# Three score tiles beside each other in four PSUM banks of one tile, key transposes at its ends, and weight conversions behind the first batch

## The chip, the core and the metric

One core of a Trainium2 chip runs the whole program. The metric is the time of one execution on the device in microseconds (us), as the median of several runs; the profile is one more execution, recorded instruction by instruction. Five engines run their own queues in order: PE (TensorE, matrix products; its weight loads are listed as PEld), DVE (VectorE), ACT (ScalarE), POOL (GpSimd) and SP, which here only issues DMAs.

## What is computed

Attention over 8 batches and 8 heads of 576 tokens with 64 features, in which only scores within `tau` of their row's maximum are kept, then a gated feed-forward layer over all 4608 tokens.

```python
scores = scale * np.matmul(q, k.transpose(0, 1, 3, 2))
thresh = np.max(scores, axis=-1, keepdims=True) - tau
scores = np.where(scores >= thresh, scores, -1000000000.0)
scores = scores - np.max(scores, axis=-1, keepdims=True)
attn = np.exp(scores)
attn = attn / (np.sum(attn, axis=-1, keepdims=True) + 1e-09)
...
gate = 1.0 / (1.0 + np.exp(-(x @ w_gate)))
val = x @ w_val
return (gate * val @ w_out).astype(np.float32)
```

All inputs are float32; `x` is the attention's output, 4608 x 512, and the weights are 512 x 1536 (twice) and 1536 x 512.

## The kernel before

**Attention** goes in 32 visits, one for each batch and pair of heads (names such as `5_1` are batch 5, pair 1). A visit has nine score tiles of 128 queries x 576 keys: four for each head and one, called `l`, for the 64 left-over queries of both heads. `tile_steps` (L571) makes one tile: PE writes the scores into a PSUM tile `s` in two halves of 288 keys (L591 for the first batch, in plain float32; L599 after it, in two or three products of split operands); DVE takes the row maximum (`st`, L606); POOL or DVE makes the threshold (L615); ACT writes the exponential of the scores into `p` (L620); DVE reads the scores again and masks `p` with the threshold, with the row sum on the side (L623). Then POOL scales `p` (L657), PE turns it in blocks (`tp`, L668; the 64 left-over keys of a group apart, `lk`, L681), ACT or DVE copies these out of PSUM (`pt` and `pl`, L630 and L631), and PE multiplies with the values (`av`, L704).

**Feed-forward.** Blocks 0, 1 and 2 run as plain products (`m`, L764, then `o`, L807) that fill PE beside the attention. The other six blocks of tokens run behind the attention in three pairs by a seven-product scheme (`q` chains at L1006, `r` chains at L1071), with three PSUM accumulators a, b and c for each chain and DVE sums at L943 and L945.

**Conversions.** The 36 weight tiles are unpacked from the host's form by POOL, ACT and DVE (`convert`, L384), written to DRAM and read again as products need them. 12 of the 24 tiles of `w_gate` and `w_val` are kept in SBUF for block 0 (`OWN`); the other 12 are read again (`wi_0a`, `wi_1a`).

**PSUM** has eight banks of 512 float32 columns for each partition. Before, `s` has two buffers of two banks each (the b accumulators of the seven-product scheme use them as well), and four single banks `b` serve everything else, `lk` among it.

**What sets the order.** The kernel first lists all operations with a priority key and a cost, and a planner (`Plan.run`) lets five queues take what is ready and has room; the resulting order is emitted as straight code. `LEAD`, `LAG`, `SHIFT`, `CONV_IN` and the costs steer it. A layer below the kernel then adds the waits: where an instruction touches a tile that an instruction of another engine has touched and the two must not overlap, the later one in the emitted order waits on a semaphore of the earlier one's engine. The planner knows buffers, but not these waits.

## Time and profile before

| what | us |
|---|---|
| three runs, median | 1356.05 |
| three runs, lowest to highest | 1355.28 to 1359.21 |
| span of the profiled execution, first to last instruction | 1352.1 |

The span leaves out what lies around it, such as the launch; against the median these are 3.95 us. Times within the profile count from the span's start. A row of a group has the line, engine, operation, tile written and tiles read, shapes, count, then busy us and mean ns of one, then the idle time ahead of it and who ended it. A row of a timeline has start, duration, engine, line, operation, and how many instructions it merges.

### The profile page before, as it was taken

How to read it: one execution, taken by the hardware profiler on the slowest of the kernel's cores; microseconds unless marked ns; L12 is line 12 of the kernel's file. 1: busy time of each engine (PE TensorE's matmuls, PEld its weight loads, DVE VectorE, ACT ScalarE, POOL GpSimd, SP SyncE). 2: the span in 40 equal slices, each digit the busy share in tenths (PEclk: the TensorE clock that was granted, in tenths of full speed). 3: DMA queues.
4: the chain of work that ended last, by engine and by line, in shares of the span. 5: the costliest groups of instructions: out<-in, count | busy, mean ns of one | idle time of the engine just before them, and what ended most of it. 6: DMA issues, size and time to landing. Idle time of an engine off the chain costs nothing.

```text
span 1352.1 us, 23686 instructions
## 1 busy us (share of the span) xinstructions
PE 1320.8 (98%) x8292; PEld 1084.1 (80%) x8292; DVE 954.8 (71%) x1943; ACT 726.9 (54%) x1339; POOL 630.3 (47%) x660
## 2 busy tenths in 40 slices
PE   7879999999999999999999999999999999999998
PEld 4557888888888888888888878888888888888887
DVE  7889868567877777778787763556965569654594
ACT  7878766666766766667776653223532225322242
POOL 6985957956777764967776741101000110001100
PEclk8989999999999999999999999999999999999999
DMA  9879999897978988898897858656695656756564
GB/s 341 279 251 309 311 257 269 233 279 209 264 212 242 261 242 227 250 267 238 238 270 188 241 179 295 205 180 211 201 308 183 201 193 204 249 180 204 186 221 129
DMA packets 140436, 317.83 MB, mean 235 GB/s; under 512 B 22048, under 2 KB 49952, under 8 KB 140320
## 3 DMA queue, kind: packets, MB, share of 16 engines
q1 hardware_dynamic: 140176, 316.33, 76.5%
q8 instruction: 67, 1.10, 0.4%
q14 instruction: 49, 0.40, 0.1%
q10 hardware_dynamic: 144, 0.00, 0.0%
HBM read 210.37 MB, written 54.53 MB: 196 GB/s over the span
## 4 chain that ended last, share of the span: by engine, by line
PE 87%; DMA 6%; DVE 2%; ACT 2%; issue 1%; POOL 1%; SPq 1%; ACTq 0%; DVEq 0%; POOLq 0%
PE m L764 13%; PE qb L1006 11%; PE av L704 11%; PE s L599 8%; PE qc L1006 7%; PE qa L1006 7%; PE tp L668 7%; PE o L807 6%; PE rb L1071 5%; PE rc L1071 4%; PE ra L1071 4%; DMA wo<-wod 2%; DMA kd<-k 2%; PE s_l L599 1%; PE lk L681 1%
## 5 line engine op out<-in xcount | busy, mean ns | idle before, releaser
L657 POOL TENSOR_SCALAR p<-p,zero_t,sm 128x576 f32<-128x576 f32 x256 | 216.3, 856 | 107.9 <-DVE sm L655 76.5
L606 DVE TENSOR_REDUCE st<-s 128x1 f32<-128x576 f32 x256 | 192.3, 754 | 91.9 <-PE s L599 83.2
L623 DVE SCALAR_TENSOR_TENSOR p<-s,st,p 128x576 f32<-128x576 f32 x256 | 205.9, 812 | 30.2 <-ACT p L620 23.9
L620 ACT ACTIVATE p<-s,st 128x576 f32<-128x576 f32 x256 | 190.2, 750 | 57.4 <-DVE st L606 56.5
L919 POOL TENSOR_TENSOR gA<-gA 128x512 f32<-128x512 f32 x18 | 24.1, 1341 | 416.2 <-DVE gA L985 416.2
L630 ACT COPY pt<-tp 128x512 f32<-128x512 f32 x256 | 147.4, 589 | 54.0 <-PE tp L668 51.9
L599 PE MATMUL s<-kd,qd 128*128 128x288 f32 x896 | 165.0, 308 | 3.7 <-issue 1.6
L668 PE MATMUL tp<-ident,p 128*128 128x128 f32 x1024 | 156.7, 282 | 2.5 <-POOL p L657 2.0
L764 PE MATMUL m<-x,wi 128*128 128x512 f32 x576 | 158.9, 403 | 0.0
L668 PEld LDWEIGHTS tp<-ident,p 128*128 128x128 f32 x1024 | 123.2, 143 | 29.4 <-POOL p L657 7.6
L599 PEld LDWEIGHTS s<-kd,qd 128*128 128x128 f32 x896 | 133.9, 190 | 14.6 <-DVE p_l L623 2.4
L704 PE MATMUL av<-pt,vs 128*64 128x256 f32 x1024 | 126.1, 389 | 0.0
L807 PE MATMUL o<-g,wo 128*128 128x512 f32 x432 | 117.5, 401 | 0.0
L943 DVE TENSOR_TENSOR qu<-qb,qp 128x512 f32<-128x512 f32 x72 | 49.8, 692 | 89.9 <-PE qb L1006 77.1
L764 PEld LDWEIGHTS m<-x,wi 128*128 128x128 f32 x576 | 99.9, 189 | 14.3
L1006 PE MATMUL qa<-xs_p,wa 128*128 128x512 f32 x432 | 109.6, 389 | 0.0
L704 PEld LDWEIGHTS av<-pt,vs 128*64 128x64 f32 x1024 | 68.6, 138 | 48.5 <-issue 7.5
L1006 PEld LDWEIGHTS qa<-xs_p,wa 128*128 128x128 f32 x432 | 81.1, 188 | 16.8
L807 PEld LDWEIGHTS o<-g,wo 128*128 128x128 f32 x432 | 75.5, 189 | 10.9
L630 ACT COPY xf<-av 128x256 f32<-128x256 f32 x64 | 25.6, 399 | 77.4 <-PE av L704 73.1
L911 ACT CAST gs_p<-gA 128x512 fp32r<-128x512 f32 x54 | 32.4, 620 | 64.5 <-DVE gA L985 26.5
L981 ACT ACTIVATE gA<-qa 128x512 f32<-128x512 f32 x18 | 10.8, 598 | 103.4 <-PE qa L1006 103.4
(148 smaller groups left out, 2628.3 us busy)
## 6 DMA issues: line engine op xcount, KB each, us to landing
kd<-k SPq DMA_DIRECT2D x112, 320.0 KB, 6.0
wi<-wid SPq DMA_DIRECT2D x48, 512.0 KB, 6.9
wo<-wod SPq DMA_DIRECT2D x36, 512.0 KB, 7.0
wa<-wid SPq DMA_DIRECT2D x36, 512.0 KB, 4.1
ws<-sid SPq DMA_DIRECT2D x36, 512.0 KB, 4.5
wt<-sid SPq DMA_DIRECT2D x36, 512.0 KB, 3.3
wo_p<-sod SPq DMA_DIRECT2D x36, 512.0 KB, 4.6
qd<-q SPq DMA_DIRECT2D x112, 128.0 KB, 4.6
```

The costliest lines, as they stand in the source:

```text
L599: nc.tensor.matmul(s.ap[:, c, :HALF], st(), mv(slice(kc + c * HALF, kc + (c + 1) * HALF)), start=m == 0, stop=m == len(steps) - 1,)
L606: op("DVE", 0.76, key, lambda: nc.vector.tensor_reduce(out=st.ap[:, 0:1], in_=sv(), axis=AX.XY, op=ALU.max, negate=True), reads=[s], write ...
L620: op("ACT", 0.74, key, lambda: nc.scalar.activation(p(), sv(), AF.Exp, bias=st.ap[:, 0:1], scale=1.0), reads=[s, (st, 0)], writes=[(g.p, i)])
L623: op("DVE", 0.9, key, lambda: nc.vector.scalar_tensor_tensor(out=p(), in0=sv(), scalar=st.ap[:, 1:2], in1=p(), op0=ALU.is_ge, op1=ALU.mult ...
L630: return op("ACT", act(n), key, lambda: nc.scalar.copy(dst(), src.ap), reads=[src], writes=[part])
L657: op("POOL", 0.9, key, lambda i=i: nc.gpsimd.tensor_scalar(out=p.ap[:, i * S : (i + 1) * S], in0=p.ap[:, i * S : (i + 1) * S], scalar1=zer ...
L668: nc.tensor.matmul(tp.ap[:, c, :], self.p.ap[:, o + c * P : o + (c + 1) * P], ident, is_transpose=True, start=c == 0, stop=c == NJ - 1, sk ...
L704: nc.tensor.matmul(av.ap[h * D : (h + 1) * D, a:z], vis.vs.ap[:, j, h], m(h), start=i == 0, stop=i == len(ms) - 1, skip_group_check=True,)
L764: nc.tensor.matmul(m.ap, wv[:, a, c * P : (c + 1) * P], xs[c].ap[:, z, c0:c1], start=e == 0, stop=e == 11,)
L807: nc.tensor.matmul(acc.ap, wv[:, f, a], g[fg * ND + f].ap[:, z], start=(fg, f, a, z) == (0, 0, 0, 0), stop=(fg, f, a, z) == (NFG - 1, ND - ...
L1006: nc.tensor.matmul(acc.ap, wv[:, y, (2 * h + c) * P : (2 * h + c + 1) * P], xt[prod][c].get()[:, z], start=e == 0 and prod in FIRST, stop= ...
L1071: nc.tensor.matmul(acc.ap, w.ap[:, e, c, y], gt[prod][2 * g + c].get()[:, z], start=m == 0 and g == 0 and prod in FIRST, stop=m == 5 and g ...
```

## The change

- PSUM: instead of two `s` buffers of two banks each, one tile `shared` of 2048 columns in four banks. A score tile takes one of three places of 576 columns, side by side from column 160 on: 160 to 736, 736 to 1312, 1312 to 1888. The first place lies in banks 0 and 1, the second in 1 and 2, the third in 2 and 3. Each tile is written in two pieces that end at a bank border (352 and 224, 288 and 288, 224 and 352 columns). The left-over key transposes `lk` go to the 128 columns at either end of `shared`; the b accumulators take whole banks of it. The planner hands out places (`settle`). Readers now see the 576 columns of a tile in one run.
- The first batch's keys are stored whole in both halves of the partitions, since a piece may now start anywhere (`k0`, `SK` columns for each tile instead of 352).
- Conversions get later keys (`CONV_IN`), all 24 tiles of `w_gate` and `w_val` stay in SBUF for block 0 (`OWN` 24, `w` 10 buffers), the second batch is put 20 tiles later in key (`SHIFT`), the scores of a visit are held behind a unit of the feed-forward layer in the planner's order (`held_by`, `RATE`, `SLACK`), and `LEAD`, `LAG` and `THR_UNTIL` have new numbers.

```diff
...
     def __init__(self, plan, tag, shape, dtype, name, cls=None):
         self.plan, self.tag, self.shape, self.dtype, self.name, self.cls = plan, tag, shape, dtype, name, cls
-        self.t, self.accesses, self.users, self.held = None, [], 0, False
+        self.t, self.accesses, self.users, self.held, self.place = None, [], 0, False, None
         self.turn = plan.made[tag] = plan.made.get(tag, 0) + 1
     @property
...
     def __init__(self, pools, slots):
         self.pools, self.slots = pools, slots
         self.ops, self.held, self.made, self.given = [], {}, {}, {}
+        self.homes, self.live = {}, {}
     def buf(self, tag, shape, dtype, name, cls=None):
         return Buf(self, tag, shape, dtype, name, cls)
     def make(self, b):
+        if b.place is not None:
+            return self.shared[:, b.place[0] : b.place[1]]
         pool, bufs = self.pools[b.tag]
         return pool.tile(b.shape, b.dtype, tag=b.tag, name=b.name, bufs=bufs)
...
                 return False
+        if not self.settle([b for s in need.values() for b in s]):
+            return False
...
+    def settle(self, bufs):
+
+        taken = list(self.live.values())
+        places = {}
+        for b in bufs:
+            if b.tag not in self.homes:
+                continue
+            n = b.shape[-1] if b.tag != "s" else self.homes["s"][0][1] - self.homes["s"][0][0]
+            for c0, c1 in self.homes[b.tag]:
+                if all(c1 <= x or y <= c0 for x, y in taken):
+                    places[b] = (c0, c1)
+                    taken.append((c0, c1))
+                    break
+            else:
+                return False
+        for b, at in places.items():
+            b.place = self.live[b] = at
+        return True
     def run(self):
         engines = ("PE", "DVE", "ACT", "POOL", "SP")
...
                     for b in x.bufs:
                         b.users -= 1
                         if not b.users and b.held:
+                            self.live.pop(b, None)
                             self.held[b.tag] -= 1
                             self.held[b.tag, b.cls] -= 1
                     for s in x.succ:
...
 SLOTS = {
     "kn": 1, "qn": 1, "vn": 1, "k2": 1, "q2": 1, "kd": 3, "qd": 3, "vs": 3,
     "p": 3, "pc": 1, "sm": 8, "st": 16, "pt": 2, "pl": 2, "ptc": 1, "plc": 1, "xf": 2, "x": 5, "g": 12,
-    "w": 8, "t2": 6,
+    "w": 10, "t2": 6,
 }
-LEAD = 8
-CONV_IN, CONV_OUT = (10, 1.5), (56, 3)
+LEAD = 7
+CONV_IN, CONV_OUT = (30, 2.5), (56, 3)
 EARLY = 16
...
     return "ACT"
-THR_FIRST, THR_UNTIL, LK_UNTIL = "POOL", 36, 300
+THR_FIRST, THR_UNTIL, LK_UNTIL = "POOL", 90, 300
 def TP(g, i):
...
-OWN = 12
-
-SHIFT = 50
+OWN = 24
+
+SHIFT = 70
 def LO_DVE(j, out):
...
 DVE_LO_IN, DVE_LO_OUT = range(18,24), ()
-LAG = {"PE": 1.2, "DVE": 0.3, "ACT": 0.08, "POOL": 0.3, "SP": 0.08}
+LAG = {"PE": 1.5, "DVE": 0.3, "ACT": 0.08, "POOL": 0.3, "SP": 0.08}
 WARM = 16
+
+RATE, SLACK = 3, 3
 FIRST_PAIRS = 4
 KD_COST = 1.2
...
     nc.vector.tensor_scalar(out=scale_t, in0=tau_t, scalar1=0.0, scalar2=QSCALE, op0=ALU.is_ge, op1=ALU.mult)
-    warm = ps.tile([P, 2, SM], F32, tag="s", name="warm")
+    shared = ps.tile([P, NJ * SM], F32, tag="shared", name="shared", bufs=1)
...
     pools = {t: (sb, n) for t, n in SLOTS.items()}
-    pools["s"], pools["b"] = (ps, 2), (ps, 4)
+    pools["s"], pools["e"], pools["q"], pools["b"] = (ps, 3), (ps, 2), (ps, 4), (ps, 4)
     slots = {t: n for t, (_, n) in pools.items()}
     active = {"att": 1, "moe": 0}
...
     last_att = [None]
     plan = Both(pools, slots)
+    plan.shared = shared
+    SIDE = (NJ * SM - 3 * S) // 2
+    plan.homes = {
+        "s": [(SIDE + i * S, SIDE + (i + 1) * S) for i in range(3)],
+        "e": [(0, P), (NJ * SM - P, NJ * SM)],
+        "q": [(i * SM, (i + 1) * SM) for i in (0, 2, 1, 3)],
+    }
     op, buf = plan.op, plan.buf
     def dram(shape, name):
...
         def plain_scores(self, key, n):
             pair = 4 * self.b + self.hp
-            self.k1 = [buf("qd", [P, HALF + SL], F32, f"kp{n}_{h}") for h in range(2)]
+            self.k1 = [buf("qd", [P, SK], F32, f"kp{n}_{h}") for h in range(2)]
             qn = self.q1 = buf("kd", [P, 2, S], F32, f"qp{n}")
             pieces = [(0, 2 * P), (2 * P, S)] if n == "0_0" else [(0, S)]
...
         n = f"{g.name}{i}"
-        s = buf("s", [P, 2, SM], F32, f"s{n}")
+        s = buf("s", [P, S], F32, f"s{n}")
         kc = SL if i == 0 else 0
-        sv = lambda: s.ap[:, :, :HALF]
+        sv = lambda: s.ap
         cols = None if h is None else slice(qt * P - vis.c0, (qt + 1) * P - vis.c0)
         if vis.plain_s:
...
             ]
             reads = [vis.qd[h], vis.kd[h]]
+        def pieces():
+            c0, c1 = s.place
+            at = -(-c0 // SM) * SM - c0
+            assert c0 + at < c1 and SL <= at and max(at, S - at) <= HALF + SL
+            return (0, at), (at, S)
+
         def plain_scores():
-            for (x, c0, r0, r1), c in itertools.product(heads, range(2)):
+            for (x, c0, r0, r1), (a, z) in itertools.product(heads, pieces()):
+                c = (s.place[0] + a) // SM % 2
                 rows = slice(c * D, (c + 1) * D)
                 nc.tensor.matmul(
-                    s.ap[r0:r1, c, :HALF], vis.q1.ap[rows, x, c0 : c0 + r1 - r0],
-                    vis.k1[x].ap[rows, kc : kc + HALF], start=True, stop=True, skip_group_check=True,
+                    s.ap[r0:r1, a:z], vis.q1.ap[rows, x, c0 : c0 + r1 - r0],
+                    vis.k1[x].ap[rows, kc + a : kc + z], start=True, stop=True, skip_group_check=True,
                 )
         def scores():
             for m, (st, mv) in enumerate(steps):
-                for c in range(2):
+                for a, z in pieces():
                     nc.tensor.matmul(
-                        s.ap[:, c, :HALF], st(), mv(slice(kc + c * HALF, kc + (c + 1) * HALF)),
+                        s.ap[:, a:z], st(), mv(slice(kc + a, kc + z)),
                         start=m == 0, stop=m == len(steps) - 1,
                     )
-        op("PE", 0.8 if vis.plain_s else len(steps) * 2 * mm(HALF), key, plain_scores if vis.plain_s else scores, reads=reads, writes=[s], also=[g.p])
+        op("PE", 0.8 if vis.plain_s else len(steps) * 2 * mm(HALF), key, plain_scores if vis.plain_s else scores, reads=reads, writes=[s], also=[g.p], after=held_by(vis))
         st = buf("st", [P, 2], F32, f"st{n}")
         op("DVE", 0.76, key, lambda: nc.vector.tensor_reduce(
-            out=st.ap[:, 0:1], in_=sv(), axis=AX.XY, op=ALU.max, negate=True
+            out=st.ap[:, 0:1], in_=sv(), axis=AX.X, op=ALU.max, negate=True
         ), reads=[s], writes=[(st, 0)])
         thr = THR(vis.first)
         if thr == "ACT":
...
                 out=st.ap[:, 1:2], in0=st.ap[:, 0:1], scalar1=-1.0, scalar2=ntau_t[:, 0:1],
                 op0=ALU.mult, op1=ALU.add,
             ), reads=[(st, 0)], writes=[(st, 1)])
-        p = lambda: g.p.ap[:, i * S : (i + 1) * S].rearrange("p (a c) -> p a c", a=2)
+        p = lambda: g.p.ap[:, i * S : (i + 1) * S]
         op("ACT", 0.74, key, lambda: nc.scalar.activation(
             p(), sv(), AF.Exp, bias=st.ap[:, 0:1], scale=1.0
         ), reads=[s, (st, 0)], writes=[(g.p, i)])
...
         if e == "ACT":
             return op("ACT", act(n), key, lambda: nc.scalar.copy(dst(), src.ap), reads=[src], writes=[part])
         return op("DVE", dve(n), key, lambda: nc.vector.tensor_copy(dst(), src.ap), reads=[src], writes=[part])
+
+    def held_by(vis):
+        n = RATE * (4 * vis.b + vis.hp - 4) - SLACK
+        return [unit_ends[n]] if 0 <= n < len(unit_ends) else []
     class Group:
...
         def leftover_keys(self, key):
-            lk = buf("b", [P, P], F32, f"lk{self.name}", "att")
+            lk = buf("e", [P, P], F32, f"lk{self.name}")
             o = SM if self.n == 2 else S - P
             op("PE", 0.14, key, lambda: nc.tensor.matmul(
                 lk.ap, self.p.ap[:, o : o + P], ident, is_transpose=True
...
     def chains(n, scale, done, tag):
-        ps_ = {c: buf("s" if c == "b" else "b", [P, SM], F32, f"{tag}{c}{n}", "moe") for c in "abc"}
+        ps_ = {c: buf("q" if c == "b" else "b", [P, SM], F32, f"{tag}{c}{n}", "moe") for c in "abc"}
         t = {c: buf("pc" if c == "u3" and not (tag == "r" and n.endswith("_1")) else "t2", [P, SM], F32, f"{tag}{c}{n}") for c in ("p1", "u2", "u3")}
         def plus(bank, x, out):
...
```

How the built program changes is shown at three places around the start of visit 5_1, in the middle of the attention. A row has the line, the operation, tile written and tiles read, the shape, and the engines whose semaphores it waits on (a wait that an earlier one covers is not repeated). The number at a name's end only counts names. `s5_1_000` is a score tile of visit 5_1 (head 0, first group, first tile), `s5_1_l40` that of its left-over queries, and `shared_84` the new PSUM tile.

DVE before, from the maximum of visit 5_1's first tile on (a maximum writes `st`, a mask `p`):

```order
L606 TENSOR_REDUCE st5_1_000_7079<-s5_1_000_7070 128x1 [waits PE_49]
L615 TENSOR_SCALAR st5_1_000_7079<-st5_1_000_7079,ntau_t_80 128x1 [waits DVE_49]
L623 SCALAR_TENSOR_TENSOR p5_0_12_7044,sm5_0_12_7055<-s5_0_121_7057,st5_0_121_7067,p5_0_12_7044 128x576 [waits Activation_49]
L655 RECIPROCAL sm5_0_12_7055<-sm5_0_12_7055 128x2 [waits DVE_49]
L623 SCALAR_TENSOR_TENSOR p5_1_00_7089,sm5_1_00_7108<-s5_1_000_7070,st5_1_000_7079,p5_1_00_7089 128x576 [waits Activation_49]
L606 TENSOR_REDUCE st5_1_001_7120<-s5_1_001_7103 128x1 [waits PE_49]
L615 TENSOR_SCALAR st5_1_001_7120<-st5_1_001_7120,ntau_t_80 128x1 [waits DVE_49]
L606 TENSOR_REDUCE st5_1_l40_7135<-s5_1_l40_7122 128x1 [waits PE_49]
```

DVE now, from the same maximum on:

```order
L647 TENSOR_REDUCE st5_1_000_6535<-shared_84 128x1 [waits Activation_49]
L664 SCALAR_TENSOR_TENSOR p5_0_12_6500,sm5_0_12_6522<-shared_84,st5_0_121_6498,p5_0_12_6500 128x576 [waits DVE_49,PE_49]
L700 RECIPROCAL sm5_0_12_6522<-sm5_0_12_6522 128x2 [waits DVE_49]
L656 TENSOR_SCALAR st5_1_000_6535<-st5_1_000_6535,ntau_t_80 128x1
L664 SCALAR_TENSOR_TENSOR p5_1_00_6550,sm5_1_00_6561<-shared_84,st5_1_000_6535,p5_1_00_6550 128x576 [waits DVE_49,Activation_49]
L647 TENSOR_REDUCE st5_1_001_6578<-shared_84 128x1 [waits PE_49]
L656 TENSOR_SCALAR st5_1_001_6578<-st5_1_001_6578,ntau_t_80 128x1 [waits DVE_49]
L647 TENSOR_REDUCE st5_1_l40_6588<-shared_84 128x1 [waits PE_49]
L656 TENSOR_SCALAR st5_1_l40_6588<-st5_1_l40_6588,ntau_t_80 128x1 [waits DVE_49]
L647 TENSOR_REDUCE st5_1_020_6598<-shared_84 128x1 [waits Activation_49]
```

The work is the same and its order nearly so; before, each maximum waits for PE, which wrote its scores; now the maxima of tiles `000` and `020` wait for ACT, and the mask of tile `5_0_121` waits for PE.

ACT before, from the copy of a transpose on (`pt` and `xf` are copies out of `b` banks, `pl` the copies of the key transposes `lk`):

```order
L630 COPY pt5_1_00_7230<-tp5_1_001_7224 128x4x128 [waits PE_49]
L823 ACTIVATE ot1_2_7266<-o1_2_6756 128x512 [waits PE_49]
L620 ACTIVATE p5_1_02_7213<-s5_1_021_7201,st5_1_021_7215 128x576 [waits DVE_49]
L630 COPY xf5_0_7180<-av5_0_12_7240 128x320 [waits PE_49]
L630 COPY pl5_1_00_7291<-lk5_1_00_7279 128x128 [waits PE_49]
L869 CAST s0_o0_1_7112<-s0_o0_1_7112 128x4x128 [waits Pool_49]
L630 COPY pt5_1_l4_7310<-tp5_1_l40_7294 128x512 [waits PE_49]
L630 COPY pl5_1_l4_7317<-lk5_1_l4_7303 128x128 [waits PE_49]
```

ACT now, from the same visit's transposes on:

```order
L671 COPY pt5_1_00_6701<-tp5_1_000_6692 128x4x128 [waits PE_49,Activation_49]
L671 COPY pt5_1_00_6701<-tp5_1_001_6703 128x4x128 [waits PE_49]
L671 COPY pl5_1_00_6721<-shared_84 128x128 [waits DVE_49,PE_49]
L671 COPY pt5_1_l4_6723<-tp5_1_l40_6712 128x512
L671 COPY pl5_1_l4_6733<-shared_84 128x128 [waits DVE_49]
L661 ACTIVATE p5_1_02_6651<-shared_84,st5_1_021_6731 128x576 [waits PE_49]
L661 ACTIVATE p5_1_10_6755<-shared_84,st5_1_100_6747 128x576 [waits DVE_49,Pool_49]
```

The copies `pl` waited for PE alone; now they wait for DVE, which does not touch the columns that they read, and the exponentials wait for PE or DVE.

PE before, the first key transposes of visit 5_1 and the scores beside them:

```order
L681 MATMUL lk5_1_00_7279<-ident_71,p5_1_00_7089 128x128 [waits Activation_49]
L599 MATMUL s5_1_100_7284<-kd5_1_1_6979,qd5_1_1_6963 128x288 [waits DMAHW3_49,DMAHW2_49,DMAHW4_49,DMAHW1_49,DVE_49]
L599 MATMUL s5_1_100_7284<-kd5_1_1_6979,qd5_1_1_6963 128x288 x3
L668 MATMUL tp5_1_l40_7294<-ident_71,p5_1_l4_7163 128x128 [waits Activation_49,Pool_49]
L668 MATMUL tp5_1_l40_7294<-ident_71,p5_1_l4_7163 128x128 x3
L681 MATMUL lk5_1_l4_7303<-ident_71,p5_1_l4_7163 128x128 [waits Activation_49]
```

PE now, the same transposes and the next scores:

```order
L726 MATMUL shared_84<-ident_71,p5_1_00_6550 128x128 [waits DVE_49,Pool_49]
L713 MATMUL tp5_1_001_6703<-ident_71,p5_1_00_6550 128x128 x4
L726 MATMUL shared_84<-ident_71,p5_1_l4_6605 128x128 [waits Pool_49]
L713 MATMUL tp5_1_l40_6712<-ident_71,p5_1_l4_6605 128x128 [waits Activation_49]
L713 MATMUL tp5_1_l40_6712<-ident_71,p5_1_l4_6605 128x128 x3
L640 MATMUL shared_84<-kd5_1_0_6294,qd5_1_0_6304 128x352
L640 MATMUL shared_84<-kd5_1_0_6294,qd5_1_0_6304 128x224
L640 MATMUL shared_84<-kd5_1_0_6294,qd5_1_0_6304 128x352
L640 MATMUL shared_84<-kd5_1_0_6294,qd5_1_0_6304 128x224
L640 MATMUL shared_84<-kd5_1_1_6400,qd5_1_1_6380 128x288 [waits DMAHW3_49,DMAHW1_49,DMAHW4_49,DMAHW0_49,Activation_49]
```

The key transposes waited for ACT, which empties the bank that they take; now the first waits for DVE. The scores waited for DVE; now they wait for ACT.

In the whole built program every access to `shared` waits, by a wait of its own or through others, for the last access ahead of it of each other engine, whatever columns the two touch.

More of the change, by code (lines that the diff above doesn't have):

```diff
@@ L353 @@
     nc.vector.tensor_scalar(out=scale_t, in0=tau_t, scalar1=0.0, scalar2=QSCALE, op0=ALU.is_ge, op1=ALU.mult)
-    warm = ps.tile([P, 2, SM], F32, tag="s", name="warm")
+    shared = ps.tile([P, NJ * SM], F32, tag="shared", name="shared", bufs=1)
     for i in range(WARM):
         nc.tensor.matmul(
-            warm[:, i % 2, :P], ident, ident, is_transpose=True, start=True, stop=True, skip_group_check=True
+            shared[:, i % 2 * SM : i % 2 * SM + P], ident, ident, is_transpose=True, start=True, stop=True, skip_group_check=True
         )
     pools = {t: (sb, n) for t, n in SLOTS.items()}
-    pools["s"], pools["b"] = (ps, 2), (ps, 4)
+    pools["s"], pools["e"], pools["q"], pools["b"] = (ps, 3), (ps, 2), (ps, 4), (ps, 4)
     slots = {t: n for t, (_, n) in pools.items()}
@@ L1265 @@
     from concourse.bass_utils import run_bass_kernel_spmd as _run
-    nc = _bacc.Bacc("TRN2", target_bir_lowering=False, num_devices=1)
+    nc = _bacc.Bacc("TRN2", target_bir_lowering=False, num_devices=1, dynamic_dma_scratch_size=4096)
     arrays, args = {}, []
```

2 lines of the change are left out of this document (1 added, 1 removed).

## The prediction

> **What bounds the kernel now.** I read the totals first, then stages of the span.
>
> ```profile
> PE 1320.8 (98%) x8292; PEld 1084.1 (80%) x8292; DVE 954.8 (71%) x1943; ACT 726.9 (54%) x1339; POOL 630.3 (47%) x660
> ...
> 0.00:101.00 101.00, 79.19 (x567) 51.60 (x568) 84.53 (x175) 77.82 (x148) 81.70 (x120) 0.90 0.85 291
> 101.00:817.00 716.00, 710.85 (x5387) 593.29 (x5385) 537.67 (x1274) 483.99 (x907) 494.37 (x501) 1.00 0.86 247
> 817.00:833.00 16.00, 16.00 (x75) 13.24 (x71) 5.25 (x5) 5.08 (x9) 5.86 (x4) 1.00 0.80 270
> 833.00:1352.00 519.00, 514.74 (x2271) 426.02 (x2270) 327.37 (x491) 160.02 (x275) 48.38 (x36) 1.00 0.63 207
> ```
>
> A row of stages has its length, the busy time of PE, PEld, DVE, ACT and POOL, PE's granted clock, and the share and GB/s of the DMA engines. PE is the bound: it works 711 of 716 us in the attention behind the first batch, and 515 of 519 behind the attention. Only the first 101 us leave it idle, for 21.8 us, and only there is its clock below 1.00. Its waits say on whom:
>
> ```profile
> PE s L591 <- DVE p L623: 13.0, 12, 2.4
> PE tp L668 <- POOL p L657: 2.0, 4, 0.7
> ```
>
> (us in total, times, longest.) The first batch's scores wait 13.0 us for masks that free one of two `s` buffers; no DMA stands in that list. So a third score buffer can win at most the idle 21.8 us, and a little from the clock.
>
> **What a score tile costs.** The groups of the tile's readers, and a stretch of the timeline:
>
> ```profile
> L623 DVE SCALAR_TENSOR_TENSOR p<-s,st,p 128x576 f32<-128x576 f32 x256 | 205.9, 812 | 30.2 <-ACT p L620 23.9 <-POOL st L615 2.0 <-POOL s L870 0.7
> L606 DVE TENSOR_REDUCE st<-s 128x1 f32<-128x576 f32 x256 | 192.3, 754 | 91.9 <-PE s L599 83.2 <-PE s L591 4.7
> ...
> L620 ACT ACTIVATE p<-s,st 128x576 f32<-128x576 f32 x256 | 190.2, 750 | 57.4 <-DVE st L606 56.5
> ...
> L630 ACT COPY pl<-lk 128x128 f32<-128x128 f32 x112 | 30.8, 275 | 1.8 <-PE lk L681 1.1
> ```
>
> ```profile
> 561.91 0.27 PE L681 MATMUL lk<-ident,p 128*128 128x128 f32 x1
> ...
> 561.94 0.77 PE L599 MATMUL s<-kd,qd 128*128 128x288 f32 x4
> ...
> 562.60 0.27 ACT L630 COPY pl<-lk 128x128 f32<-128x128 f32 x1
> 562.75 0.76 DVE L606 TENSOR_REDUCE st<-s 128x1 f32<-128x576 f32 x1
> 562.76 1.53 ACT L620 ACTIVATE p<-s,st 128x576 f32<-128x576 f32 x2
> ...
> 576.95 0.76 DVE L606 TENSOR_REDUCE st<-s 128x1 f32<-128x576 f32 x1
> ...
> 577.75 0.74 ACT L620 ACTIVATE p<-s,st 128x576 f32<-128x576 f32 x1 [0.20 <-DVE st L606]
> ```
>
> Writing a tile takes PE 0.77 us from its first product to the last result, then follow 0.754 (maximum), 0.750 (exponential) and 0.812 (mask): 3.09 us in a row. It does not show today because tiles overlap: at 562.75 DVE takes the maximum of one tile in the very time that ACT works on another, and ACT copies `lk` while PE writes scores. A hand-over costs 0.04 us (the maximum ends at 577.71, ACT starts at 577.75).
>
> **What the change does to that.** It puts all these tiles into one, and the rows of the built program show the price: DVE's maxima of tiles `000` and `020` wait for ACT, whose instructions read other places; the copies of key transposes wait for DVE; scores wait for ACT. In the whole program each access to `shared` is behind the last earlier access of every other engine. Up to the last mask I counted 1126 turns in which one engine after the other touches it: PE 313, DVE 457, ACT 356. So PE, DVE and ACT are never in it together, and the attention becomes one chain.
>
> **The chain, by turns.** For a visit: nine tiles of 3.09 us, 27.8; five key transposes with their copies, 5 x (0.27 + 0.275) = 2.7; 1126 / 32 = 35.2 hand-overs of 0.04, 1.4; less some 0.5 where PE writes two tiles in one turn and the second streams. That is 31.4 us, and 32 visits are 1005 us. Today the last mask is already done at 805:
>
> ```profile
> 804.16 0.81 DVE L623 SCALAR_TENSOR_TENSOR p<-s,st,p 128x576 f32<-128x576 f32 x1
> ```
>
> **Waits in the queues** come on top, since each engine also has other work between its turns, in an order fixed for engines that overlap. Queued behind a waiting PE are transposes, `av` and the feed-forward products; behind DVE the sums, thresholds and splits; behind ACT all copies. I walked visit 5_1 through the built order with the rows' durations, and it takes 37.0 us for 38 turns instead of 32.4. The 4.6 us are places such as these: a mask behind the split of the next queries (1.37 us on DVE), an exponential behind their scaling (0.84 on ACT), a key transpose behind two value products (2.90 on PE):
>
> ```profile
> L521 DVE SCALAR_TENSOR_TENSOR q<-qn,scale_t,q 128x640 fp32r<-128x640 f32 x28 | 38.3, 1370 | 3.8 <-ACT q L516 2.7
> ...
> L516 ACT ACTIVATE q<-qn,scale_t 128x640 fp32r<-128x640 f32 x28 | 23.4, 837 | 0.0
> ...
> 309.06 2.90 PE av L704 x44
> ```
>
> By turns, the mean visit has 37.0 x 35.2 / 38 = 34.2, and 32 visits 1094 us. Two terms I estimate: 25 us in batch 1, where most conversions now meet the chain (73 more DVE operations of about 0.69 us than in other batches, 50 us, half of them in DVE's idle time), and 25 us for PE's clock. At 78% busy PE has 0.90 above; here its work up to the last mask, 79 + 711 us less the 250 products that move behind (57 us), fills 64% of 1150, so 313 turns of 0.77 become about 0.08 longer. With 6 us before the first maximum the last mask is at 1150.
>
> **Behind the chain.** 322 products of the plain blocks now stand on PE behind the last mask, by the built order (72 behind the last `av` today), at
>
> ```profile
> 1339.59 8.17 PE rc L1071 x36
> ```
>
> 8.17 / 36 = 0.227 us: 73 us, with the last transposes and `av` 78. The three pairs of blocks follow with 2268 products, 515 us, which no wait interrupts today; output after the last product adds 4.3. Their b accumulators share `shared` too. In the first half 18 or 6 products lie between two writes there, more than the DVE sums between them need; in the second half 12 DVE reads have none, and PE waits for 0.692 + 0.04 and some 0.17 of its own last product, 11 us in all:
>
> ```profile
> L943 DVE TENSOR_TENSOR qu<-qb,qp 128x512 f32<-128x512 f32 x72 | 49.8, 692 | 89.9 <-PE qb L1006 77.1 <-ACT gs_p L911 8.9 <-ACT gs_p_q L911 2.2
> ```
>
> So 78 + 515 + 4 + 11 = 608. The span becomes 1150 + 608 = 1758, and with the 3.95 us by which the median stands above the span, about **1762**.
>
> **The other edits** I cost at nothing. The twelve loads and their waits on the SP queue go with `wi_0a` and `wi_1a`, but PE waits for no load today; if a load were late, the chain's idle PE covers it. `THR_UNTIL` moves no operation: the first batch starts at tiles 0 to 27 and the second at 106 (86 before), on the same sides of 36 and 90. `LEAD` 7 prepares a visit seven tiles ahead, some 20 us at today's pace and more at the new one, against 11.76 us for its slowest load on the chain of waits; if the cover were gone, the difference to eight tiles is 2.8 us a visit:
>
> ```profile
> 290.32 11.76 DMA kd<-k
> ```
>
> Whole `k0` rows add 144 KB to each of eight early loads, at the first stage's 291 GB/s half a us, once on the path. The pacing of visits is an order on PE, and is in the 322.
>
> **Rivals.** *The overlap survives, and PE waits less* (not slower). It decides if engines may read and write different places at once, or if the order leaves turns so far apart that no one waits. Then the first stage loses up to its 21.8 us of waits, the rest stays at PE's pace, and the time is between 1325 and 1380, about 1335. For it: DVE and ACT are idle 29% and 46% of the span. Against it: the waits in the rows hold places without a common column. 6%.
>
> The Trainium skill, PSUM — Partial Sum Buffer, section "PSUM bank collisions raise a hardware error", says that two engines must be kept apart only within one bank and the same partitions. By that, the first and the third place would be free of each other, and of three successive tiles two would exclude each other: 2 x 3.09 for three tiles, 18.5 us a visit, below today's 805 / 32 = 25.2, so PE would stay the bound, which is this rival. The order's rows disagree: the copies of the end columns wait for masks of any place.
>
> *The chain alone* sets the pace, since the queues' other work fits into the waits: 31.4 x 32 + 6 + 25 for the clock, 1036, + 608 + 4 gives 1648. For it: visits without conversions have only some 16 other DVE operations. Against it: the walked visit. 12%.
>
> *PE's clock falls much further.* An early tile shows what that costs, here at 1.18 us against 0.76 for the same kind later:
>
> ```profile
> 9.96 1.18 PE L591 MATMUL s<-kp,qp 64*128 64x288 f32 x4
> ...
> 17.43 0.76 PE L591 MATMUL s<-kp,qp 64*128 64x288 f32 x4 [1.81 <-DVE p L623]
> ```
>
> 0.42 on 313 turns is 131 us: about 1890. For it: PE will be idle a third of the time. Against it: with waits of up to 2.4 us the first stage kept 0.90. 10%.
>
> The Trainium skill, TensorE: Matmul & The Clock Gate, section "Why this matters for your kernels", puts the limit at idle gaps of about 3 us; by that rule this rival needs gaps above the longest in the walked visit, 2.3 us.
>
> **How the numbers follow.** My forecast, chain plus queue waits, has 72%, with 1660 to 1880 of its own, since one walked visit carries it. The chain alone has 12, the clock 10, the surviving overlap 6. The range, 1620 to 1900, holds the forecast and the chain alone, reaches into the clock's case, and leaves out the overlap. About 0.3% can be told from no change: faster 0.05 and within 0.01 are the overlap's, slower 0.94 is the rest.
>
> **What would show it.** Right: the last masks near 1150 us, not 805; PE's longest waits at score writes for DVE and ACT; idle time of DVE's maximum ended by ACT, of ACT's `pl` copies by DVE; PE busy some 64% before and over 95% behind; the last 520 us unchanged but for 11. Wrong: a maximum and an exponential at the same time on different tiles, or an attention that ends by 850.

## The result and the profile after

The changed kernel takes 1753.43 us (median of four runs, 1752.11 to 1757.02), the kernel before beside it 1356.26 (1355.28 to 1359.21). The ratio is 1.2932, with a 95% interval of 1.2905 to 1.2959: slower by 29%, 397 us.

The profiled execution has a span of 1752.4 us. First the totals of its page, then PE's busy time and granted clock in 40 slices of the span, each digit a tenth:

```profile
PE 1458.7 (83%) x8292; PEld 1137.8 (65%) x8292; DVE 962.5 (55%) x1953; ACT 734.2 (42%) x1329; POOL 630.7 (36%) x660
...
PE   5666998777777777777767777899999999999998
...
PEclk9777999899989999998999999899999999999999
```

The number of products is the same, 8292, but no engine is the bound any more: PE went from 98% to 83%, DVE from 71 to 55, ACT from 54 to 42. For two thirds of the span PE works some 7 tenths of the time. The stages, cut at the last mask and where the plain blocks are nearly done (length, then busy time of PE, PEld, DVE, ACT, POOL, the clock, DMA):

```profile
0.00:101.00 101.00, 63.27 (x302) 35.27 (x302) 40.50 (x87) 40.37 (x72) 35.41 (x61) 0.85 0.41 142
101.00:1136.00 1035.00, 794.52 (x5318) 611.23 (x5318) 579.01 (x1354) 508.72 (x938) 494.11 (x517) 0.92 0.57 164
1136.00:1210.00 74.00, 71.84 (x364) 58.20 (x364) 20.99 (x25) 24.75 (x44) 52.77 (x47) 0.99 0.69 243
1210.00:1752.00 542.00, 529.01 (x2313) 433.13 (x2311) 322.03 (x488) 160.37 (x276) 48.42 (x36) 1.00 0.62 203
```

Nearly all of the loss arises ahead of 1136 us; what stands behind it takes longer than before (616 us against 547) because products that the attention left over are done there. Ahead of 1136 us PE is idle for 278 us; before, it was idle 22 of the first 101 and 5 of the next 716. That is 251 of the span's 400 us, and 11 more are idle time behind. The other 138 are PE's own busy time, which grew from 1320.8 to 1458.7 us for the same products. Up to the last mask, 162 us of PE's work now lie in short stretches at half the clock (19 before), and its products come in 267 separate runs (44 before). How much each of the two adds was not taken apart.

Which waits the idle time consists of, the groups of the readers and writers of score tiles tell. Their last numbers are the idle time ahead of them and what ended most of it:

```profile
L647 DVE TENSOR_REDUCE st<-shared 128x1 f32<-128x576 f32 x256 | 193.3, 756 | 261.5 <-ACT p L661 99.0
L661 ACT ACTIVATE p<-shared,st 128x576 f32<-128x576 f32 x256 | 188.3, 742 | 263.7 <-DVE st L647 95.0
L664 DVE SCALAR_TENSOR_TENSOR p<-shared,st,p 128x576 f32<-128x576 f32 x256 | 207.3, 814 | 157.3 <-ACT p L661 59.1
L640 PE MATMUL shared<-kd,qd 128*128 128x352 f32 (+2 forms) x896 | 185.4, 338 | 109.5 <-DVE st L647 43.3
...
L671 ACT COPY pl<-shared 128x128 f32<-128x128 f32 x104 | 27.6, 266 | 148.6 <-PE shared L640 52.8
```

The durations are those of before (maximum 756 ns against 754, exponential 742 against 750, mask 814 against 812). What grew is the waiting: the maximum from 91.9 to 261.5 us, and while PE's scores ended 83 of its 92 us before, the largest share is now ended by ACT's exponential. That pair is the sign looked for: a maximum reads only the scores of its own tile, so an exponential that it waits for belongs to another place. PE's own list of waits (us in total, times, longest):

```profile
PE shared L726 <- DVE p L664: 61.9, 45, 4.3
PE shared L640 <- DVE st L647: 51.3, 52, 2.2
PE shared L726 <- ACT p L661: 30.4, 20, 3.2
...
PE shared L1116 <- DVE ru L990: 4.7, 6, 0.8
```

L726 writes key transposes, and tops the list: it waits for masks and exponentials, whose columns of `shared` it never touches. A stretch of the timeline in the middle of the attention, where `[0.40 <-ACT pl L671]` is idle time ahead and what ended it:

```profile
602.46 0.79 PE L640 MATMUL shared<-kd,qd 128*128 128x288 f32 x4 [0.40 <-ACT pl L671]
...
603.36 0.76 DVE L647 TENSOR_REDUCE st<-shared 128x1 f32<-128x576 f32 x1 [3.05 <-PE shared L640]
...
604.15 0.27 ACT L671 COPY pl_l<-shared 128x128 f32<-128x128 f32 x1 [1.25 <-DVE st L647]
...
604.47 0.81 PE L640 MATMUL shared<-kd,qd 128*128 128x224 f32 x4 [0.78 <-ACT pl_l L671]
...
605.38 0.76 DVE L647 TENSOR_REDUCE st<-shared 128x1 f32<-128x576 f32 x1 [1.02 <-PE shared L640]
...
606.23 0.74 ACT L661 ACTIVATE p<-shared,st 128x576 f32<-128x576 f32 x1 [1.33 <-DVE st L647]
```

Read down: PE, then DVE, ACT, PE, DVE, ACT, and each starts where the one above it ends. The scores written at 604.47 go to a place of their own, yet had to wait for a copy of 128 columns at the tile's end. Counted over the whole trace, ACT's exponentials run 109.9 of their 215.5 us beside a maximum or mask of DVE before the change, and 0.0 of 213.6 us after it.

### The profile page after: what moved, and what is told of

Read it like the earlier page. It is cut to its first block, busy times and chain, and to the rows that moved or that the text cites. A ratio compares the mean times of both kernels' runs of the same rounds, so it can differ in the third digit from the quotient of the medians.

```text
span 1752.4 us, 23686 instructions
## 1 busy us (share of the span) xinstructions
PE 1458.7 (83%) x8292; PEld 1137.8 (65%) x8292; DVE 962.5 (55%) x1953; ACT 734.2 (42%) x1329; POOL 630.7 (36%) x660
## 5 line engine op out<-in xcount | busy, mean ns | idle before, releaser
L647 DVE TENSOR_REDUCE st<-shared 128x1 f32<-128x576 f32 x256 | 193.3, 756 | 261.5 <-ACT p L661 99.0
L661 ACT ACTIVATE p<-shared,st 128x576 f32<-128x576 f32 x256 | 188.3, 742 | 263.7 <-DVE st L647 95.0
L664 DVE SCALAR_TENSOR_TENSOR p<-shared,st,p 128x576 f32<-128x576 f32 x256 | 207.3, 814 | 157.3 <-ACT p L661 59.1
L640 PE MATMUL shared<-kd,qd 128*128 128x352 f32 (+2 forms) x896 | 185.4, 338 | 109.5 <-DVE st L647 43.3
L640 PEld LDWEIGHTS shared<-kd,qd 128*128 128x128 f32 x896 | 141.3, 207 | 151.3 <-DVE st L647 51.6
L713 PE MATMUL tp<-ident,p 128*128 128x128 f32 x1024 | 170.5, 297 | 0.1
L671 ACT COPY pt<-tp 128x512 f32<-128x512 f32 x256 | 146.6, 587 | 49.9 <-PE tp L713 48.6
L726 PE MATMUL shared<-ident,p 128*128 128x128 f32 x128 | 42.7, 333 | 122.0 <-DVE p L664 52.4
L988 DVE TENSOR_TENSOR qu<-shared,qp 128x512 f32<-128x512 f32 x72 | 49.8, 691 | 144.5 <-PE shared L1051 106.9
L726 PEld LDWEIGHTS shared<-ident,p 128*128 128x128 f32 x128 | 18.8, 147 | 148.0 <-DVE p L664 46.1
L671 ACT COPY pl<-shared 128x128 f32<-128x128 f32 x104 | 27.6, 266 | 148.6 <-PE shared L640 52.8
```

What stands on the lines that cost most here:

```text
L640: nc.tensor.matmul(s.ap[:, a:z], st(), mv(slice(kc + a, kc + z)), start=m == 0, stop=m == len(steps) - 1,)
L647: op("DVE", 0.76, key, lambda: nc.vector.tensor_reduce(out=st.ap[:, 0:1], in_=sv(), axis=AX.X, op=ALU.max, negate=True), reads=[s], writes ...
L661: op("ACT", 0.74, key, lambda: nc.scalar.activation(p(), sv(), AF.Exp, bias=st.ap[:, 0:1], scale=1.0), reads=[s, (st, 0)], writes=[(g.p, i)])
L664: op("DVE", 0.9, key, lambda: nc.vector.scalar_tensor_tensor(out=p(), in0=sv(), scalar=st.ap[:, 1:2], in1=p(), op0=ALU.is_ge, op1=ALU.mult ...
L671: return op("ACT", act(n), key, lambda: nc.scalar.copy(dst(), src.ap), reads=[src], writes=[part])
L713: nc.tensor.matmul(tp.ap[:, c, :], self.p.ap[:, o + c * P : o + (c + 1) * P], ident, is_transpose=True, start=c == 0, stop=c == NJ - 1, sk ...
```

## The experiments

Each diff is against the changed kernel unless it says otherwise. A run "beside" gives the median of the kernel before on the same chip.

### Two places, a framework tile for each

`e1_two_tiles` takes the third place and the transposes out of `shared`, and makes a tile of each pair of banks. All new planner numbers stay.

```diff
-            return self.shared[:, b.place[0] : b.place[1]]
+            i, c = b.place[0] // 1024, b.place[0] // 1024 * 1024
+            return self.shared[i][:, b.place[0] - c : b.place[1] - c]
...
-    shared = ps.tile([P, NJ * SM], F32, tag="shared", name="shared", bufs=1)
+    shared = [ps.tile([P, 2 * SM], F32, tag=f"shared{i}", name=f"shared{i}", bufs=1) for i in range(2)]
...
-        "s": [(SIDE + i * S, SIDE + (i + 1) * S) for i in range(3)],
-        "e": [(0, P), (NJ * SM - P, NJ * SM)],
+        "s": [(SM - HALF + i * 2 * SM, SM + HALF + i * 2 * SM) for i in range(2)],
...
-            lk = buf("e", [P, P], F32, f"lk{self.name}")
+            lk = buf("b", [P, P], F32, f"lk{self.name}", "att")
```

> Two score places (columns 224 to 800 and 1248 to 1824, no common bank), each pair of banks a tile of its own; key transposes back in a single bank b; all the new planner numbers and conversions kept. Theory (one PSUM tile is used by one engine at a time, whatever the columns): the chain is gone, PE is the bound again, 1335 to 1375 us, attention done near 800. Rival A (the new numbers, the later conversions and the pacing of visits make the loss): 1600 or more, like the change. Rival B (uneven pieces of 352 and 224 columns across bank borders make it): 1335 to 1375 as well, told apart by the next run.

Measured: 1364.5 us beside 1355.3, ratio 1.0067 (1.004 to 1.0094). 389 of the 397 us are gone. The overlap is back as well: exponentials run 114.1 us beside work of DVE.

### The same two places in one framework tile

`e2_one_tile` is `e1_two_tiles` with one declaration changed, so that both places belong to one tile again. The instructions and their order are the same on every engine; only the waits differ.

```diff
-    shared = [ps.tile([P, 2 * SM], F32, tag=f"shared{i}", name=f"shared{i}", bufs=1) for i in range(2)]
+    shared = ps.tile([P, NJ * SM], F32, tag="shared", name="shared", bufs=1)
```

> The same program as the run before in the same order on every engine; only the two pairs of banks are one PSUM tile, so only waits differ. Theory: 909 turns of one engine after the other up to the last mask, nine tiles of 3.09 us and 28 hand-overs a visit are 28.9 us, with queue waits about 33, last mask near 1060, 1640 to 1710 us. Rival B (uneven pieces) and rival C (engines are kept apart by bank, not by tile): no bank is common to the two places, so within 1% of the run before.

Measured: 1581.4 us, 217 more than with two tiles. PE's longest entries for score tiles, with two tiles and then with one:

```profile
PE shared L631 <- DVE p L663: 15.9, 14, 2.6
```

```profile
PE shared L638 <- DVE p L662: 47.5, 48, 3.0
PE shared L638 <- DVE st L645: 32.1, 56, 1.3
PE shared L630 <- DVE p L662: 24.6, 16, 3.9
PE shared L638 <- ACT p L659: 19.4, 24, 1.4
```

The new waits are for maxima and exponentials, and the overlap of exponentials with DVE falls from 114.1 to 0.0 us. The two places lie in different banks (columns 224 to 800 and 1248 to 1824), so waits between them cannot come from a shared bank: the tile as a whole is what is kept apart, and **that costs 217 us with nothing else changed**. The size was expected too high; how much the products behind the chain decide of it is seen with the two outer places, below.

### The key transposes back in `b`

```diff
-            lk = buf("e", [P, P], F32, f"lk{self.name}")
+            lk = buf("b", [P, P], F32, f"lk{self.name}", "att")
```

> The change with the key transposes back in a single bank b; three places of one tile. Theory: 880 turns instead of 1126 and 2.7 us less work in the chain of a visit, about 33 us a visit, 1640 to 1710 us. Rival D (the transposes at the ends of the tile, which wait longest on PE, are what costs): most of the loss goes, 1400 to 1500 us.

Measured: 1663.4 us, 90 less than the change, with the last mask at 1045 instead of 1136. 246 turns of the chain are gone (1126 to 880). The prediction's own terms, five transposes with their copies at 2.7 us a visit and the hand-overs, give 32 x 2.7 + 246 x 0.04 = 96. The transposes are a quarter of the loss, and not the main cause (one execution).

### The old planner numbers under the new tile

`e4_old_numbers` sets `LEAD`, `CONV_IN`, `THR_UNTIL`, `OWN`, `SHIFT`, `LAG` and `w` back and lets `held_by` hold nothing.

> The new PSUM tile with the old numbers: 12 kept in-weights, 8 w buffers, conversions from key 10 on, second batch at key 86, no pacing of visits, old lead and lags. Theory: 1127 turns as in the change; the last mask near 1150 and fewer plain products behind it, so 1690 to 1770 us. Rival A (the numbers make the loss): 1340 to 1380 us.

Measured: 1766.4 us. The loss is there without any of the new numbers.

### The new conversion numbers alone, and the pacing alone

Both start from the kernel before. `e5_conversions` has its two tiles `s` and the change's `w` 10, `CONV_IN`, `THR_UNTIL`, `OWN` and `SHIFT` (and a smaller scratch area for DMAs, so that the two buffers more fit). `e6_pacing` has `LEAD`, `LAG`, `RATE`, `SLACK`:

```diff
-LEAD = 8
+LEAD = 7
...
-LAG = {"PE": 1.2, "DVE": 0.3, "ACT": 0.08, "POOL": 0.3, "SP": 0.08}
+LAG = {"PE": 1.5, "DVE": 0.3, "ACT": 0.08, "POOL": 0.3, "SP": 0.08}
...
+RATE, SLACK = 3, 3
...
-        op("PE", 0.8 if vis.plain_s else len(steps) * 2 * mm(HALF), key, plain_scores if vis.plain_s else scores, reads=reads, writes=[s], also=[g.p])
+        op("PE", 0.8 if vis.plain_s else len(steps) * 2 * mm(HALF), key, plain_scores if vis.plain_s else scores, reads=reads, writes=[s], also=[g.p], after=held_by(vis))
```

> The kernel before with the new conversion numbers alone (later keys, 24 kept in-weights, 10 w buffers, second batch at key 106, thresholds until 90); own score tiles, old pacing. It and the next two ask where the 0.67% come from by which two tiles with all new numbers are slower than before (1364.5 against 1355.3). If the conversions behind the first batch make them: 1361 to 1368 us. If the pacing or the tile's form does: 1352 to 1358 us.

> The kernel before with the new pacing alone (lead 7, PE lag 1.5, scores of a visit held behind a unit of the feed-forward layer). If the pacing makes the 0.67%: 1361 to 1368 us, with the last mask nearer 830 than 804. If not: 1352 to 1358 us.

Measured: the conversion numbers 1356.8 us, ratio 1.0012 (0.9991 to 1.0033), no difference; the pacing 1366.9, ratio 1.0078 (1.005 to 1.0106). It costs about 10 us by itself, as much as the whole excess of `e1_two_tiles` (9 us). Part of it shows in the stage behind the first batch, in the kernel before and then with the pacing (same columns as the stages above):

```profile
101.00:300.00 199.00, 196.75 (x1409) 163.57 (x1408) 151.91 (x347) 138.50 (x263) 141.77 (x141) 1.00 0.95 275
```

```profile
101.00:300.00 199.00, 193.08 (x1394) 160.62 (x1394) 150.18 (x338) 136.77 (x260) 140.32 (x140) 1.00 0.88 269
```

PE is idle 5.9 us instead of 2.3 here.

### The tile form alone

`e7_tiles_only` is `e1_two_tiles` with all old numbers: places, `settle`, whole `k0` rows and `q` accumulators over four banks remain of the change.

> The kernel before with two score tiles of 576 neighbouring columns in their own two banks each, whole keys in the first batch and the b accumulators in four banks of these two tiles; all old numbers. If the form of the tile or the longer key loads make the 0.67%: 1361 to 1368 us. If not: 1352 to 1358 us.

Measured: 1355.5 us, ratio 1.0004 (0.9983 to 1.0024). None of this costs anything that can be measured.

### Plain products brought ahead of the last mask

The change leaves 322 plain products for the time behind its last mask. `e8_rate4` lets the planner hold a visit's scores behind more of them:

```diff
-RATE, SLACK = 3, 3
+RATE, SLACK = 4, 4
```

> The change with visits held behind later units (4 a visit instead of 3), so that 26 plain products stand behind the last mask instead of 324. Theory: the chain leaves PE idle, so the 298 products (68 us) fit into it at a cost of 0 to 30 us of chain: last mask 1136 to 1165, 1685 to 1715 us. Rival E (products behind the attention are no loss, as PE has no time for them ahead): 1745 to 1765 us.

Measured: 1761.3 us, 8 more than the change: the theory fails, the rival holds. Six products are left behind the last mask, but that mask comes at 1206 instead of 1136. The stage up to 1136 us, in this kernel:

```profile
101.00:1136.00 1035.00, 809.74 (x5300) 629.62 (x5297) 546.99 (x1271) 497.83 (x923) 516.90 (x536) 0.93 0.59 175
```

PE is busier by 15 us than in the change's row of the same stage, and DVE, which does the chain's maxima and masks, by 32 us less busy. PE works in order, so a run of products longer than the other engines' turns holds up its own next turn. Estimated over the built order with the durations of the rows, PE's products exceed the gaps that they stand in by 24 us in the change and by 80 us here, 56 of the 70 us by which the mask is late. The traces agree: of the time between the end of another engine's turn and PE's next one, PE spends 23 us on other products in the change and 75 us here. Idle PE time in a chain takes products only where they fit.

### The two outer places

`e3_lk_in_b` (three places, 1663.4 us) and `e2_one_tile` (two, 1581.4) differ in the third place and in how the bank borders cut the tiles. `e10_outer_places` takes the middle place out of the former; its order is that of `e2_one_tile` on every engine, and only its pieces are 352 and 224 columns instead of twice 288.

```diff
-        "s": [(SIDE + i * S, SIDE + (i + 1) * S) for i in range(3)],
+        "s": [(SIDE + i * S, SIDE + (i + 1) * S) for i in (0, 2)],
```

> The kernel with three places and the transposes in `b` (measured at 1663 us, last mask at 1045, 320 plain products behind it), with the middle place taken out: two places left, at columns 160 to 736 and 1312 to 1888, still in one framework tile, each still cut in pieces of 352 and 224 columns by a bank border. 909 accesses of the chain, as in the two-place kernel in one tile (1581 us, last mask at 1026, 12 plain products behind it), whose pieces are 288 and 288. Theory: what the third place costs beside that is that the planner writes score tiles further ahead and leaves products for the end, so without it 1570 to 1595 us, some 12 plain products behind the last mask. Rival: the uneven pieces cost it: 1640 to 1670 us.

Measured: 1596.2 us, 1.2 above the theory's range and far from the rival's. The masks of both kernels (count, shortest, median and longest in ns, first and last start), with three places and with two:

```profile
L663 DVE SCALAR_TENSOR_TENSOR p<-shared,st,p x256: 795/817/821, 13.4 to 1045.0; 128x576 f32<-128x576 f32 x128
```

```profile
L663 DVE SCALAR_TENSOR_TENSOR p<-shared,st,p x256: 795/816/820, 11.3 to 1040.5; 128x576 f32<-128x576 f32 x128
```

The attention ends within 5 us of each other, but with three places 316 plain products are still to come, and with two 11: 305 x 0.227 = 69 us, and the kernels differ by 67. A third place in a chain gives no overlap; what it gives is an order with scores further ahead and products further behind. Here these products do fit: the same estimate as for `e8_rate4` gives 24 us of excess with two places and 30 with three, and the traces show 26 us in both. So a chain of two places comes out at some 1590 us and not at the 1640 and more expected for it, which is what three places take. The uneven pieces cost the remaining 15 us (1596.2 against 1581.4). That is one execution each, where the kernel before scatters over 9 us, but PE's turns in the two chains differ by 12 us (260 against 247).

### Key transposes beside score tiles, in two tiles

`e9_lk_beside` is the one part of the change not yet tried by itself, and the candidate for a gain: `e7_tiles_only` with the transposes in free columns at the outer end of each tile.

```diff
-            lk = buf("b", [P, P], F32, f"lk{self.name}", "att")
+            lk = buf("e", [P, P], F32, f"lk{self.name}")
...
+        "e": [(0, P), (NJ * SM - P, NJ * SM)],
```

> The two-place kernel with the old numbers (two framework tiles, one for each pair of banks, measured at 1355.5 us) with one thing more: the transposes of k's last rows are written into free columns at the outer end of each tile and not into a buffer of `b`. Accesses of one tile wait for each other, those of the two tiles do not. Theory: the price of lying beside score tiles is paid only where the chain of a tile is the bound. With two tiles each chain takes some 3.1 us for two visits' worth of alternate tiles, less than PE's work in the same time, so the second tile hides most of it: 1352 to 1375 us, the last mask at 805 to 840 us. Rival (a buffer of `b` that comes free lets PE go on sooner): 1352 or less. Rival (lying beside is dear in itself, as the 90 us between the change and the same with these transposes in `b` might be read): 1400 or more.

Measured: 1388.6 us beside 1356.8, ratio 1.0242 (1.0217 to 1.0267), with the last mask at 839 us instead of 803. The mask is where the theory put it, but the time misses all three ranges: more than the theory's 1375, less than the rival's 1400. Without it and with it, behind the first batch:

```profile
101.00:805.00 704.00, 699.07 (x5287) 585.00 (x5286) 536.38 (x1269) 480.19 (x901) 489.53 (x500) 1.00 0.86 248
```

```profile
101.00:805.00 704.00, 685.32 (x5096) 562.29 (x5095) 512.18 (x1214) 471.17 (x878) 480.77 (x491) 1.00 0.83 242
```

14 us of it are new idle time of PE (4.9 to 18.7). In the first 101 us PE is idle as long in both. The rest, some 19 us, is no waiting: PE's busy total is 20 us longer (1340.7 against 1320.6) for the same 8292 products, with a clock of 0.83 instead of 0.92 in the first 101 us. Which part of it the clock is, and which the smaller bunches of products, wasn't taken apart. So lying beside score tiles costs even where the second tile could hide the chain, a third of what it costs with one tile (90 us).

Set in a row, the runs lead from the kernel before to the change: the new numbers with two tiles add 9 us, one tile in place of two 217, the uneven pieces 15, the third place 67, and the transposes beside the score tiles 90, together 398 of the 397 us. The three kernels between `e1_two_tiles` and the change were executed once each.

No version tried is faster than the kernel before. One was not tried: waits kept by bank instead of by tile, which would leave the first and third places free of each other. It needs other waits from the layer below, or each score tile written and read in pieces of one bank. The Trainium skill, PSUM — Partial Sum Buffer, section "PSUM bank collisions raise a hardware error", asks for that separation within one bank and the same partitions; no run here let two engines into one bank at the same time.

## Why the prediction was right

It gave 1762 us in 1620 to 1900; measured were 1753.43. Its mechanism is shown by the pair `e1_two_tiles` and `e2_one_tile`. By its steps:

- **Turns.** "PE, DVE and ACT are never in it together": the overlap of exponentials with DVE's maxima and masks is 0.0 us, and the trace has the 1126 turns that were counted in the built order (PE 313, DVE 457, ACT 356). The walked visit 5_1 was to take 37.0 us and takes 37.1 from last mask to last mask.
- **The last mask** was put at 1150. In the trace:

```profile
1135.59 0.81 DVE L664 SCALAR_TENSOR_TENSOR p<-shared,st,p 128x576 f32<-128x576 f32 x1
```

- Its **terms** were off in both directions, and that the last mask came within 14 us is in part luck. Counted from a turn's first start to its last end, the turns of DVE and ACT take 712 us in the trace, as the sum has them (451 + 260). PE's take 317, where the sum has 249 for the products, 25 for the clock and 6 for the start: 37 too few. Between one turn's end and the next one's start pass 105 us, where it has 45 for hand-overs, 89 for waits in the queues and 25 for batch 1: 54 too many. The two errors largely cancel. Part of PE's excess is the clock: 98 PE turns of four score products at full clock take 0.80 us in the mean, and 17 in stretches at half the clock 1.38.
- **By batches**, from the trace's last masks, batches 2 to 7 take 34.3 us a visit, where the sum had 34.2 and 0.8 for the clock. Batch 1 has 38.4 a visit, 16 us above that pace instead of 25. The first batch has 39.6, which is 21 us beside the later pace, instead of 6 for the start. Sum: 32 x 34.3 + 16 + 21 = 1135.
- **Two signs** missed. PE was to be busy some 64% before the last mask and is busy 76% (858 of 1136 us), since its own work grew as said above. ACT's `pl` copies were to wait for DVE; of the idle time ahead of them PE's scores end 68 us, and DVE's masks and maxima 59.
- **Behind the chain** 608 were expected; from 1136.4 us to the end it is 616. On the chain of waits (start, duration, what):

```profile
1202.18 5.85 DMA wo<-wod
1208.08 12.91 PE o L852 x48
1220.99 1.36 PE qa L1051 x6
...
1351.71 5.45 PE shared L1116 x24
1357.93 3.06 PE shared L1116 x12
```

The plain products end at 1220.99, 84.6 us behind the last mask instead of 78; 2.2 of this is a wait for the load of `wo`, a DMA that the prediction costed at nothing. From there it is 531.4 us, where 515 + 4.3 + 11 gives 530. The gap between the last two rows, 1357.16 to 1357.93, is one of the 12 stalls of the b accumulators: 0.77 us, for 0.9 in the sum, and PE's list of waits has 4.7 + 2.4 for DVE and 2.5 without a releaser, 9.6 us in all.

- **"The other edits I cost at nothing"**: shown for the conversion numbers and the form of the tiles, wrong for the pacing. It was taken as an order on PE that counts only in the 322 products behind the chain; alone it costs 10 us where there is no chain, and 3.7 of these are seen as idle time of PE behind the first batch.
- **The 322 products** as a loss of 73 us of their own: it held as part of the sum, but `e8_rate4` shows that it isn't one that can be taken back alone, and `e10_outer_places` that another order can.
- **The rivals.** The surviving overlap (1335) fell, and with it the idea that engines wait only where columns or banks are common: in `e2_one_tile` neither is. The chain alone (1648) lacks the waits in the queues, which the walked visit had. The clock's case (1890) did not come, as the last section shows.

## What to carry to other kernels

Before several buffers are put into one PSUM tile, look at what the waits go by: here each access waited for the last one of every other engine anywhere in the tile, reads behind reads too, and that turned three overlapping engines into a chain, at 217 us for one declaration. In the profile such a chain is seen at once by unchanged durations of the readers, a smaller busy share of every engine, and readers that wait for readers of another place. More places in such a tile bought nothing here, and what an engine in order has to do between its turns is free only where it fits into the gap.

## What was not expected of the hardware

PE's clock gave way less than feared, and in short stretches. The slices between 44 and 175 us are granted 0.7 of full speed, and single transposes show it. A key transpose behind a wait of 3.21 us, and one in the middle of the attention behind 1.31 us:

```profile
83.70 0.48 PE L726 MATMUL shared<-ident,p 128*128 128x128 f32 x1 [3.21 <-ACT p L661]
```

```profile
607.03 0.33 PE L726 MATMUL shared<-ident,p 128*128 128x128 f32 x1 [1.31 <-ACT p L661]
```

Without a wait ahead of it the same transpose takes 0.27 us. The trace has ten waits of PE above 2.7 us, six of them in the first 101 us, which goes with a granted clock of 0.85 there and 0.92 behind; that also bears on the first batch's 39.6 us a visit. The 0.85 counts the first 47.5 us as full speed, for which the trace holds no clock record; transposes at 27.39 and 36.16 us take 0.47 as well.

These times follow the clock granted at that moment, and not the length of the wait. Of the 157 key transposes behind the clock's first record, the 137 that start at full clock take 0.27 to 0.33 us, one behind a wait of 3.34 us among them, and the 20 that start in a stretch at half the clock take 0.42 to 0.48. One of the 20 stands behind a wait of only 2.27 us; it, and the stretch around it (length, busy times, and as the third number from the end the clock):

```profile
119.61 0.47 PE L726 MATMUL shared<-ident,p 128*128 128x128 f32 x1 [2.27 <-DVE st L647]
```

```profile
119.20:125.90 6.70, 4.98 (x23) 2.10 (x25) 2.11 (x5) 1.64 (x5) 3.38 (x5) 0.50 0.46 157
```

The Trainium skill, TensorE: Matmul & The Clock Gate, section "Why this matters for your kernels", puts the limit at idle gaps of about 3 us. The trace does not bear this out: between 101 us and the last mask it has 29 stretches at half the clock, of 3.4 to 17.1 us, but only four waits above 2.7 us. In the 3.4 us ahead of one of 13.7 us, which begins at 504.9, the longest wait is 2.33 us, and ahead of one of 10.2 us at 1122.7 it is 1.47. What all 29 share is that PE is busy at most 59% of the 3.4 us ahead of them; whether that decides was not tested. Together they last 160 us, and so an engine that is idle a quarter of the time kept nine tenths of its clock.
